# The second product of the MLP in seven half-size products, for the second chunk of the second to sixth batch too

## The chip, the core and the metric

The kernel runs on one NeuronCore of a Trainium2 chip. The core has five engines, each with its own in-order queue: TensorE (PE, matrix products and transposes, with its weight loads listed as PEld), VectorE (DVE), ScalarE (ACT), GpSimd (POOL) and SyncE (SP), which here only issues DMAs. Matrix products land in PSUM, a small memory from which DVE and ACT read, and everything else lives in SBUF. The metric is the device time of the kernel in microseconds (us). Every run is set against the median of the kernel before, 1778.69 us.

## What is computed

Two blocks, one after the other, all in 32-bit floating point.

```python
# top-k attention: 8 batches, 8 heads, 576 rows, head size 64
scores = scale * q @ k.T
kth    = 32nd largest score of each row
scores = where(scores >= kth, scores, -1e9)
x      = softmax(scores) @ v            # heads side by side: (8, 576, 512)

# Fourier mix and MLP
u  = x + real(fft(fft(x, axis=1), axis=2))
un = (u - mean(u)) / sqrt(var(u) + 1e-6)
out = u + relu(un @ w_ch1) @ w_ch2      # 512 -> 2048 -> 512
```

## The kernel before

**The main loop.** The attention works on tiles of 128 rows of one head (and one tile of 64 rows of both heads); there are 9 tiles for a pair of heads, 36 for a batch and 288 in all. The main loop (from L1589) makes one *program step* for a tile, so a batch is a round of 36 steps. In step i PE makes the scores of tile i+3, DVE finds the top 32 of tiles i and i+1 (four MAX8 and three MATCH_REPLACE8 on 576 columns for each tile, L446 and L448), POOL writes the tile's bounds (`nt`, L455), ACT and POOL mask the tile before (L469, L472), ACT takes the exponential (L480) and splits it in two planes (L493), SP writes the planes to DRAM and brings them back transposed (`PT`, L506 and L527), and PE multiplies them with v some steps later (`attend`, L585). What a step issues is put on each engine's queue in the order of the program, and no engine overtakes itself.

**The rest of a batch** runs under the attention of the next two. Take batch b. In steps 3 to 9 of the next round POOL folds its x (`near`, L762, is the last). In steps 10 and 12 PE makes the transform over tokens (`dft_tokens`, tile `yp`, L809), in steps 13 and 14 that over channels (`dft_channels`, tile `mp`, L860 and L864), and in steps 15 to 17 it transposes the normalised rows (`channels_first`, tile `tpu`, L948). ACT copies each of these out of PSUM (L834 to L847, L874, L951). From step 18 on the MLP of the batch is dealt out.

**The MLP as units.** `mlp_units` (L1041) makes a list of units: for each of two chunks of rows (chunk 0: tiles 0, 1 and the small tile 4, 320 rows; chunk 1: tiles 2 and 3, 256 rows) 16 units of the hidden layer (`hidden`, L1055, ACT writes `hT`, L1059), and then the second product. Each unit has a cost in us that the program gives it: 8 x rows / 1200 for a hidden unit, 1.75 for a part of the second product. When a batch's units arrive, `level` (L1562) looks for the step length at which what is free in the steps up to the next arrival holds all the units in the list; each step then takes units from the list, between its fixed work, up to that length (`some`, L1579). The units of a batch end just before the next arrival, in step 16 or 17 of the round after.

**The second product** has two forms. The *plain* form (`back`, L1075) takes a tile of 128 rows at a time: eight parts, each of two matrix products of 128 x 128 with 128 x 512, into a PSUM tile `cp` (L1082). For tile 2, ACT scales the result (L1108) and POOL adds it to x (L1110); for tile 3, DVE does both (L1096). The *seven-product* form (`fast`, L1155) treats two tiles together as a 2 x 2 matrix of blocks and replaces eight block products by seven (p1 to p7), each in two parts of four matrix products with 256 columns (`product`, L1254), into two PSUM tiles `cv` (p2, p5, p3) and `cw` (p1, p4, p6, p7). It needs sums of blocks. Those of the weights lie in DRAM and are brought into two quarters of the weight tile by `bring` (L976) as each product finishes, and the last two loads put the weights back. Those of `hT` are made as the products go along by `mix` (L1198): four mixes of two halves each, 128 x 512, in place in `hT`. The first mix is queued ahead of the products, the other three after p1 and p4. Results are scaled by ACT (L1225) and added by POOL (L1227), the last ones of each tile by DVE (L1211).

**Who does the sums, and when.** Mixes and adds go to a list `sums`. Up to the last tile they run on POOL. A step takes from the list what fits into 2.1 us less what is planned for POOL, then writes the bounds of its tile, and then takes what fits into another 1.3 us (`some_sums`, L1002). A planned fold counts 1.5 us, a mix 1.25. A product that needs a mix that was not yet issued issues it on the spot (`need`, L1009).

**PSUM banks.** `bank` (L144) turns three banks of the pool `ps_m`. A tile asked for with `hold` keeps its bank until its `free` is called; the others go round in what is left. Hidden units, `yp`, `mp` and `tpu` take a bank each without holding it (only in the last batch do `yp`, `mp` and `tpu` go to other pools); `cp`, `cv` and `cw` hold theirs. A plain tile's bank is freed when its result was read; `cv` is freed with DVE's add after p3, `cw` with that after p7.

```python
    def bank(shape, name, hold=False):
        n = banks_free.pop(0)
        t = ps_m.tile(shape, F32, name=name, tag=f"m{n}", bufs=1)
        if not hold:
            banks_free.append(n)
            return t
        return t, lambda: banks_free.append(n)
```

Before the change, the first batch has the plain form in both chunks, the second to sixth batch the seven products in the first chunk and the plain form in the second, and the last two batches the seven products in both. The small tile 4 is always plain.

Of the kernel before, what the change touches and what calls it, by code (L numbers as in the profile page):

```python
# [86 lines left out]
def kernel(  # L87
# [10 lines left out]
    B, H, S, D = q.shape  # L98
# [942 lines left out]
    def mlp_units(b):  # L1041
# [4 lines left out]
        def hidden(ch, it):  # L1046
            w, unT = CW[ch], unT_of[b, ch]
            if ch not in hTs:
                hTs[ch] = batp.tile([P, NIT, CW[0]], F32, name=f"hT_{b}_{ch}", tag="hT")
                hT_of[ch] = hTs[ch].rearrange("p i c -> p (i c)")[:, 0:NIT * w].rearrange(  # L1050
                    "p (i c) -> p i c", c=w
                )
            hp = bank([P, CW[0]], f"hp_{b}_{ch}_{it}")
            for dt in range(NDT):
                nc.tensor.matmul(  # L1055
                    hp[:, 0:w], lhsT=w1[:, dt, P * it:P * (it + 1)], rhs=unT[:, dt, 0:w],
                    start=(dt == 0), stop=(dt == NDT - 1),
                )
            nc.scalar.activation(out=hT_of[ch][:, it, :], in_=hp[:, 0:w], func=AF.Relu)  # L1059
# [275 lines left out]
        for ch in range(2):  # L1335
            units += [
                (8 * CW[ch] / 1200.0, lambda ch=ch, it=it: hidden(ch, it), ("hidden", b, ch))
                for it in range(NIT)
            ]
            seven = b and ch == 0 or b >= B - 2  # L1340
            if seven:
                begin, products = fast(ch)
                if ch == 0:
                    begins.append(begin)
                else:
                    units.insert(1 - NIT, (0.0, begin, ("hidden", b, 1)))
                mix_first = products.pop(0)
                units.append(mix_first)
            for t in [t for t in CHUNKS[ch] if t == 4 or not seven]:
                units += [  # L1350
                    (1.75, lambda ch=ch, t=t, p=p: back(ch, t, p), "back")
                    for p in range(4 if t == 4 else 8)
                ]
            if seven:
                units += products
# [127 lines left out]
    for b in range(B):  # L1483
# [49 lines left out]
        at(s + 1, "begin" if quick else "dve", lambda b=b: rsqrt(b))  # L1533
        arrivals.append(s + (1 if quick else 3))
        at(arrivals[-1], "units", lambda b=b: (queue if b else waiting).extend(mlp_units(b)))

    queue, waiting, pending, written, now, out_next = [], [], [], set(), [0], []
    step_us = 6.0

    def chunk_at(i):  # L1540

        for tile in (i - 5, i - 4, i - 3, i - 2):
            r = tile % PER_PAIR
            if PER_BATCH <= tile < N and r in (4, 8):
                if i - tile == ((5 if r == 4 else 4) if by_dma(tile) else 2 if tile in (2 * PER_BATCH - 1, N - 1) else 3):
                    return tile // PER_PAIR, r // 8
        return None, None
# [41 lines left out]
    while i < N + 5 or plan or queue or sums:  # L1589
# [96 lines left out]
        pair, ch = chunk_at(i)  # L1686
# [81 lines left out]
```

## Time and profile before

| | |
|---|---|
| median of 3 runs | 1778.69 us (1776.69 to 1779.95) |
| the profiled execution's own time | 1780.27 us |
| its span, first to last instruction | 1778.5 us |
| mean granted TensorE clock | 0.964 |
| PE, DVE, ACT, POOL busy | 1632.1, 1552.5, 1278.8, 906.6 us |
| one round in the steady state (1094 to 1287 us) | 193 us: PE 190.0, DVE 185.1, ACT 154.9, POOL 103.5 us busy |

The profile is of one execution. A group of instructions is shown as line, engine, operation, out<-in with sizes, count, then busy time, the mean duration of one in ns, and the idle time of the engine just before these with what ended it. A row of the timeline has start, duration, engine, line and count, and in brackets the engine's idle time before it. A matrix product in 32-bit floating point stands as two records in the trace. Busy time of a stage is read from windows given in us from the start of the span.

### The profile page before, as it was taken

To read this page: it belongs to the slowest core of one execution; us is meant where nothing else is said; L and a number is where in the kernel's file an instruction comes from. 1 tells how busy PE (TensorE), PEld (TensorE's weight loads), DVE (VectorE), ACT (ScalarE), POOL (GpSimd) and SP (SyncE) were. 2 spreads that over 40 slices of the span, in tenths; PEclk is the share of its full clock that TensorE was granted. 3 is DMA by queue.
4 is the path that set the end of the run, shared out by engine and by line. 5 is a ranking of instruction groups with operands and counts; after the bars stand their busy time and mean duration, and the time that the engine had idled before them with its cause. 6 is when DMAs were issued, how large, how long until landed. Compare 5 with 4: busy or idle time off the path is not lost.

```text
span 1778.5 us, 26295 instructions
## 1 busy us (share of the span) xinstructions
PE 1632.1 (92%) x7830; PEld 1040.9 (59%) x7830; DVE 1552.5 (87%) x3319; ACT 1278.8 (72%) x3136; POOL 906.6 (51%) x1268
## 2 busy tenths in 40 slices
PE   5666689999898989999999999999999999999998
PEld 3444455464455755566555755576566755577777
DVE  7999989999999999998999999999999999863121
ACT  6888759887787878876888778877978787653200
POOL 4768846655634565354544665356535564333000
PEclk7778799999999999999999999999999999999999
DMA  5333126651457855586557856595558655643151
GB/s 156 115 102 117 32 81 163 185 152 50 119 145 196 222 131 135 136 233 161 135 136 200 212 133 140 152 240 145 152 132 222 182 135 128 172 114 101 36 180 60
DMA packets 492926, 255.28 MB, mean 144 GB/s; under 512 B 364528, under 2 KB 483056, under 8 KB 492784
## 3 DMA queue, kind: packets, MB, share of 16 engines
q1 hardware_dynamic: 489008, 243.80, 52.5%
q0 software_dynamic: 2816, 9.44, 1.6%
q8 instruction: 63, 1.03, 0.2%
q14 instruction: 79, 0.65, 0.1%
q10 hardware_dynamic: 960, 0.36, 0.1%
HBM read 99.79 MB, written 84.74 MB: 104 GB/s over the span
## 4 chain that ended last, share of the span: by engine, by line
PE 48%; DVE 16%; ACT 16%; POOL 14%; issue 5%; DMA 2%; POOLq 0%; SPq 0%; DVEq 0%; ACTq 0%
PE hp L1055 18%; DVE m L446 7%; DVE wk L448 6%; PE o L585 6%; PE cw L1254 5%; POOL wk L472 5%; PE cv L1254 4%; PE sp L422 4%; ACT wk L469 3%; POOL fold L696 3%; PE cp L1120 2%; ACT wk L493 2%; PE cp L1082 2%; ACT S L425 2%; PE sp_t L392 1%
## 5 line engine op out<-in xcount | busy, mean ns | idle before, releaser
L472 POOL TENSOR_TENSOR wk<-S,wk 128x576 f32<-128x576 f32 x288 | 407.6, 1415 | 418.1 <-ACT wk L469 417.2
L446 DVE MAX8 m<-wk 128x8 f32<-128x576 f32 x864 | 617.4, 741 | 0.1
L1055 PE MATMUL hp<-unT,w 128*128 128x256 f32 (+1 forms) x2048 | 529.6, 409 | 6.8 <-ACT hT L1059 6.0
L1055 PEld LDWEIGHTS hp<-unT,w 128*128 128x128 f32 x2048 | 378.0, 191 | 112.0 <-ACT hT L1059 11.4
L448 DVE MATCH_REPLACE8 wk<-m,wk 128x576 f32<-128x576 f32 x576 | 424.8, 737 | 0.0
L469 ACT ACTIVATE wk<-S,nt 128x576 f32<-128x576 f32 x288 | 224.3, 779 | 96.8 <-POOL nt L455 96.3
L493 ACT COPY wk<-S 128x576 uint16<-128x576 uint16 x468 | 290.2, 673 | 0.0
L446 DVE MAX8 m<-S 128x8 f32<-128x576 f32 x288 | 214.5, 745 | 11.6 <-ACT S L396 11.6
L480 ACT ACTIVATE S<-wk,nt 128x576 f32<-128x576 f32 x234 | 185.1, 791 | 46.7 <-POOL wk L472 45.4
L448 DVE MATCH_REPLACE8 wk<-m,S 128x576 f32<-128x576 f32 x288 | 212.5, 738 | 0.0
L1082 PE MATMUL cp<-w,hT 128*128 128x512 f32 x448 | 206.0, 598 | 0.0
L1059 ACT ACTIVATE hT<-hp 128x320 f32<-128x320 f32 (+1 forms) x256 | 104.1, 411 | 140.7 <-PE hp L1055 139.7
L585 PE MATMUL o<-PT,v 128*64 128x256 f32 (+3 forms) x1440 | 196.1, 417 | 5.6 <-DVE wk L448 2.1
L422 PE MATMUL sp<-kT,qT 64*128 64x512 f32 (+1 forms) x528 | 160.1, 668 | 6.7 <-ACT S L414 3.6
L585 PEld LDWEIGHTS o<-PT,v 128*64 128x64 f32 x1440 | 113.2, 154 | 84.1 <-issue 24.8
L425 ACT COPY S<-sp 128x512 f32<-128x512 f32 (+1 forms) x264 | 141.7, 589 | 26.2 <-PE sp L422 25.2
L455 POOL TENSOR_TENSOR nt<-m,cc 128x2 f32<-128x2 f32 x288 | 58.7, 204 | 166.9 <-DVE m L446 160.4
L1254 PE MATMUL cw<-w,hT 128*128 128x256 f32 x512 | 119.7, 383 | 9.1 <-ACT ct L1225 6.2
L1082 PEld LDWEIGHTS cp<-w,hT 128*128 128x128 f32 x448 | 81.3, 193 | 75.1 <-issue 74.7
L392 PEld LDWEIGHTS sp_t<-kt,qT 128*128 128x128 f32 x320 | 51.7, 195 | 111.4 <-issue 73.3
L1254 PEld LDWEIGHTS cw<-w,hT 128*128 128x128 f32 x512 | 94.5, 190 | 27.3 <-ACT ct L1225 8.4
L1254 PE MATMUL cv<-w,hT 128*128 128x256 f32 x432 | 100.4, 383 | 6.6 <-DMA w<-w_parts 2.8
(155 smaller groups left out, 2036.3 us busy)
## 6 DMA issues: line engine op xcount, KB each, us to landing
planes<-wk SPq DMA_DIRECT2D x208, 288.0 KB, 2.7
w<-w_parts SPq DMA_DIRECT2D x94, 512.0 KB, 4.7
space<-in_moe_w_ch_dram SPq DMA_DIRECT2D x32, 512.0 KB, 3.6
nat<-in_q_dram SPq DMA_DIRECT2D x128, 64.0 KB, 2.3
v<-in_v_dram SPq DMA_DIRECT2D x32, 256.0 KB, 3.4
nat<-in_k_dram SPq DMA_DIRECT2D x62, 128.0 KB, 2.8
planes<-wk SPq DMA_DIRECT2D x52, 144.0 KB, 2.7
w_parts<-w_t POOLq DMA_DIRECT2D x8, 512.0 KB, 4.0
```

Of the source, the lines that this page charges most:

```text
L422: nc.tensor.matmul(sp[r], lhsT=qT[hd, q_cols], rhs=kT[hd, :], start=True, stop=True)
L425: nc.scalar.copy(out=s_t[r, keys], in_=sp[r])
L446: ops.append(lambda src=src, m8=m8: nc.vector.max(out=m8, in_=src))
L448: ops.append(lambda src=src, m8=m8: nc.vector.match_replace(w, m8, src, NEG))
L469: nc.scalar.activation(out=w, in_=Ssb[i], func=AF.Relu, scale=-FAR, bias=Nt[i][:, 1:2])
L472: nc.gpsimd.tensor_tensor(out=w, in0=Ssb[i], in1=w, op=ALU.subtract)
L480: nc.scalar.activation(out=Ssb[i] if by_dma(i) else w, in_=w, func=AF.Exp, bias=Nt.pop(i)[:, 0:1], accum_out=den_t[pair % 3][:, c:c + 1],)
L493: nc.scalar.copy(out=words[:, half, :], in_=src[:, half, :])
L585: nc.tensor.matmul(o[D * e:D * (e + 1), c0:c1], lhsT=vv[:, e, c, :], rhs=pt[:, NF if c == NF else (NF + 1) * e + c, c0:c1], start=(c == 0) ...
L1055: nc.tensor.matmul(hp[:, 0:w], lhsT=w1[:, dt, P * it:P * (it + 1)], rhs=unT[:, dt, 0:w], start=(dt == 0), stop=(dt == NDT - 1),)
L1082: nc.tensor.matmul(cp, lhsT=hT[:, it, P * n:P * (n + 1)], rhs=w2[:, it, :], start=(it == 0), stop=(it == NIT - 1),)
L1254: nc.tensor.matmul(dst, lhsT=h()[a][:, kc, :], rhs=rhs_of(kc), start=start and kc == 0, stop=kc == NK - 1, skip_group_check=True,)
```

## The change

One condition in `mlp_units` is changed. It decides for which chunks the seven-product form is used: before, for the first chunk of every batch but the first and for both chunks of the last two; after, for both chunks of every batch but the first. So the second chunk of the second to sixth batch changes form. Everything that `fast` issues for a second chunk comes with it: the loads at its start, placed after the chunk's first hidden unit, the first mix ahead of the products, the fourteen parts in place of sixteen, and the scratch room for scaled results in the unused end of `hT`.

```diff
@@ -1337,7 +1337,7 @@
                 (8 * CW[ch] / 1200.0, lambda ch=ch, it=it: hidden(ch, it), ("hidden", b, ch))
                 for it in range(NIT)
             ]
-            seven = b and ch == 0 or b >= B - 2
+            seven = b > 0
             if seven:
                 begin, products = fast(ch)
                 if ch == 0:
```

## The prediction

> **What bounds the kernel now.** I read the page first, for the shape of the whole span.
>
> ```profile
> PE 1632.1 (92%) x7830; PEld 1040.9 (59%) x7830; DVE 1552.5 (87%) x3319; ACT 1278.8 (72%) x3136; POOL 906.6 (51%) x1268
> ...
> PE   5666689999898989999999999999999999999998
> ...
> DVE  7999989999999999998999999999999999863121
> ...
> PEclk7778799999999999999999999999999999999999
> ```
>
> Two engines are nearly full from the sixth slice to the thirty-fifth, and PE alone after that. Which of them sets the pace is read from the busy time in single rounds of 193 us (one attention batch each), then in the 55 us in which the plain second chunk of the fifth batch runs.
>
> ```profile
> 1094.00:1287.00 193.00, 189.99 (x921) 118.70 (x920) 185.07 (x398) 154.86 (x379) 103.49 (x151) 1.00 0.65 168
> 1287.00:1480.00 193.00, 189.72 (x920) 118.60 (x919) 185.30 (x399) 154.18 (x378) 103.59 (x151) 1.00 0.65 166
> 1232.00:1287.00 55.00, 54.46 (x254) 28.00 (x253) 53.14 (x117) 48.01 (x122) 33.34 (x46) 1.00 0.56 142
> ```
>
> The columns are length, then busy time of PE, weight load, DVE, ACT and POOL, then clock. PE is idle 3.0 us of 193, DVE 7.9. The rounds repeat each other, so a steady state is reached. DVE's timeline says what its idle time is:
>
> ```profile
> 1222.01 0.42 DVE L630 TENSOR_TENSOR x<-tpx,rd 128x256 f32<-128x256 f32 x1 [0.58 <-PE tpx L626]
> ...
> 1257.85 0.76 DVE L446 MAX8 m<-S 128x8 f32<-128x576 f32 x1 [1.59 <-ACT S L396]
> ```
>
> Both are waits for work that PE issued (a transposed tile, a score block that ACT copies). So PE's in-order queue sets the round, and DVE meets it at a handful of places. A microsecond taken from or put into PE's queue counts, until DVE's 7.9 us are used up.
>
> **What the change takes away.** The groups by line give the arithmetic.
>
> ```profile
> L1082 PE MATMUL cp<-w,hT 128*128 128x512 f32 x448 | 206.0, 598 | 0.0
> ...
> L1254 PE MATMUL cw<-w,hT 128*128 128x256 f32 x512 | 119.7, 383 | 9.1 <-ACT ct L1225 6.2
> ...
> L1254 PE MATMUL cv<-w,hT 128*128 128x256 f32 x432 | 100.4, 383 | 6.6 <-DMA w<-w_parts 2.8
> ```
>
> A record costs PE 206.0/448 = 0.460 us at 512 columns and (119.7+100.4)/944 = 0.233 us at 256. The plain chunk is 64 records, 29.4 us; seven products are 7x16 = 112, 26.1 us. That is -3.3 us a batch, -16.6 us in five.
>
> **What it adds beside PE's path, a batch.** Eight POOL mixes of 1.28 us (62.5/49, L1198) and five adds of 0.73, less one add of 1.27: +12.6 us on POOL, busy 33.3 of the 55 us above. Five ACT scalings of 0.47 less one of 0.77: +1.6 us, into 48.0 of 55. On DVE a 256-wide add, +0.47 us, inside its 7.9. Twelve 512 KB loads: the SP queue spends about 0.6 us on one, 7 us a batch, and DMA is 0.56 busy there. I cost all this at nothing; the cover is those idle shares. The loads wait on SP for a product to end, with plane writes and transposes queued behind, but the operands are wanted two program steps (10 us) later. If a cover went, the dearest row is 2.8 us, PE's wait for w<-w_parts (once, second batch). The last store is issued one step later, so the four held transposed tiles go out in steps 22 to 25 instead of 20 to 24; four buffers hold them: nothing, at most DVE's longest wait there, 3.2.
>
> **Where the units fall.** The step level is that at which what is free in the 36 steps holds the batch's units. These cost 120.9 by the code's figures (34.1+27.3 hidden, 7 tail, 24.5, 28) and 117.4 after, so it falls by 0.1, from 5.24 to 5.14 us. Dealt out by hand, right to about one unit, the second chunk's hidden layer ends in step 6 with the first mix queued there; p2, p2, p5 in step 7; p5, p1 in 8; p1 in 9; p4 in 10; p4, p6 in 11; p6, p3 in 14; p3 in 15; p7, p7 in 16. That is the stretch of the next batch's token and channel transforms and the folds on POOL.
>
> **First wait added: p5 for the mix.** In the first chunk four tail units stand between the mix and p5; here only p2 does. POOL is late in these steps:
>
> ```profile
> 1236.58 0.19 POOL L455 TENSOR_TENSOR nt<-m,cc 128x2 f32<-128x2 f32 x1
> ...
> 1242.01 0.19 POOL L455 TENSOR_TENSOR nt<-m,cc 128x2 f32<-128x2 f32 x1
> ...
> 1248.21 2.14 POOL L762 TENSOR_TENSOR near<-fold 128x513 f32<-128x513 f32 x2
> ```
>
> These are the bounds of tiles 6 and 7. A step with a fold leaves room for one 1.25 us mix, behind the bounds. So the second mix half starts at 1242.2 plus 0.45 (the first half took a gap of 0.89) and ends at 1243.9. PE, from 1221.8: six hidden units of 1.77, a transpose of 0.5, score blocks 1.4, three product parts of 1.85, scores 1.4, is ready at 1241.3. It waits 2.7 us. One unit earlier or later gives 2.9 or 3.1 by the same sum; the lower end is 0.4, POOL's share in the first chunk. I take 2.7.
>
> **Second wait added: one bank.** `bank` has three PSUM banks. The plain chunk holds one at a time; seven products hold two (v from p2 to p3's add, w from p1 to p7's). In steps 8 to 16 the transforms then turn in a single bank: PE may not write the next group before ACT has read the last. The trace shows such a turn, hidden units right after p7 while both banks are held:
>
> ```profile
> 1191.02 1.89 PE L1055 MATMUL hp<-unT,w 128*128 128x256 f32 x8
> 1193.47 1.99 PE L1055 MATMUL hp<-unT,w 128*128 128x256 f32 x8 [0.56 <-ACT hT L1059]
> ```
>
> and how late ACT reads the transforms today, where a second bank hides it:
>
> ```profile
> 1252.54 0.51 PE L809 MATMUL yp<-fs,near 128*128 128x145 f32 x2
> ...
> 1254.86 0.38 ACT L834 COPY y<-yp 128x256 f32<-128x256 f32 x1
> ...
> 1255.57 0.43 ACT L834 COPY y<-yp 128x256 f32<-128x256 f32 x1
> ```
>
> The second half of the transform starts at 1252.5; ACT's reads of the first half end only as the second copy starts, 1255.6. With one bank that is a wait of 3.1. The same reading of the other adjacent pairs gives 2.5 (second token transform), 1.6 (channel transforms), 0.7, 1.6 and 0.4 (transposes): 10.0 in sum, the upper end. The lower end is ACT ready at once: twice 0.8, 0.8, 0.7, sum 3.1; a gain is excluded, as no bank is won. Walked on with PE already late by p5's wait: the transform's first half ends at 1255.5, ACT comes to it after score copies and xT at 1256.7, reads to 1257.4, wait 2.0; then ACT has caught up, 0.9, 0.9, 0.8 and none. 4.6, nearer the lower end because a late PE gives ACT time. Last, p6 follows p4 at once in the same bank: 0.6, as in the 0.56 of p4 after p1.
>
> **Sum.** -3.3 + 2.7 + 4.6 + 0.6 = +4.6 us a batch in the steady state (fourth to sixth batch: 13.8). The third keeps some idle time, 3.5. In the second, PE already idles 5.3 us in that stretch (2.96, 1.77, 0.58), half of which the new waits fill: 2.2. Total +19.5. The profiled execution took 1780.3, 1.6 above the median of 1778.7; on the median this is **1798**.
>
> **A rule weighed.** Around 826.7 the trace shows the clock at half for 3.4 us after PE idled 2.10 us, while idles of 2.8 and 3.0 us at 560 and 657 left it at 1.00.
>
> ```profile
> 826.70:830.10 3.40, 3.40 (x16) 1.77 (x14) 3.40 (x9) 0.82 (x3) 0.00 (x0) 0.51 0.52 83
> ```
>
> One such drop costs 1.7 us; one in three waits over 2 us, two of them a batch, adds 1.1 a batch, 6 in all. The Trainium skill, "TensorE: Matmul & The Clock Gate", section "Part 1: The HAM clock gate", says the clock halves only after a whole idle window of about 3.4 us. By that rule the waits above cost no clock; the 2.10 us row does not agree with it.
>
> **The rivals.**
> - *ACT stays late.* The bank waits are the 10.0 of today's alignment, p5's is 3.1, a clock drop adds 1.1: -3.3+3.1+10.0+0.6+1.1 = 11.5 a batch, with the same discounts (a factor of 0.85) +49: 1828. For it: ACT is 48 of 55 busy there. Against: ACT's own delays come partly from PE, which is late too.
> - *One bank costs nothing.* ACT reads in time; -3.3+2.7+0.6 = 0 a batch: 1779. Against: the copy at 1254.86. The Trainium skill, same page, section "HAM oscillation", reports a kernel in which PSUM double-buffering added nothing; by it this would be the outcome. The trace here disagrees at that copy.
> - *Faster.* The mixes come in time (0.4) and the banks cost 0.5 in all: -2.4 a batch, 1767. It decides where the new waits sum to less than 3.3 us, so that PE idles under 6.3 us a round. For it: seven products in the first chunk idle PE only about 1 us. Against: no transform runs there, and tails cover the mix.
>
> **Chances.** Forecast 0.62, ACT late 0.20, one bank free 0.09, faster 0.09. About 0.2% (3.6 us) is what a measurement tells from no change, so slower 0.82, same 0.09, faster 0.09. The forecast's own range, with waits of 6 to 10 us in place of 7.9, is 1790 to 1807; for 8 in 10 the range reaches to most of the late case and to the edge of no change: 1783 to 1830.
>
> **What would show it.** PE idle before the transforms (yp, mp, tpu), ended by ACT's y and us copies; PE before cv ended by POOL hT in steps 7 to 9; PE idle of about 11 us a round instead of 3; DVE's wait for S near step 12 grown by about 4 us; PE busy down 16 us. The prediction is wrong if the transforms show no wait, if the hold of the banks is shorter than read, or if PE's waits are made good because DVE or POOL paced the round.

## The result, and the profile after

The changed kernel takes 1821.02 us (median of 6 runs, 1815.97 to 1822.61) against 1779.32 us for the one before on the same chip (6 runs): a ratio of 1.0232 with a 95% interval of 1.0217 to 1.0247. That is 41.7 us slower. The forecast was slower, by 19.5 us, with 1821 inside its range; the rival "ACT stays late" had 1828.

From here on a difference between two traces is between profiled executions: span 1817.2 us after, 1778.5 before, so 38.7 us. The first line of the page after, and its groups of the products and of the mixes:

```profile
PE 1625.4 (89%) x8070; PEld 1089.5 (60%) x8070; DVE 1555.5 (86%) x3324; ACT 1291.1 (71%) x3156; POOL 965.9 (53%) x1328
...
L1254 PE MATMUL cw<-w,hT 128*128 128x256 f32 x832 | 198.8, 385 | 11.7 <-ACT ct L1225 4.2
...
L1254 PE MATMUL cv<-w,hT 128*128 128x256 f32 x672 | 163.3, 391 | 26.4 <-POOL hT L1198 9.2
...
L1198 POOL TENSOR_TENSOR hT<-hT 128x512 f32<-128x512 f32 x89 | 113.4, 1275 | 11.6 <-PE cw L1254 11.6
```

PE's busy time fell by 6.7 us and its idle time grew by 45.4 (span less busy: 146.4 before, 191.8 after). The forecast had -16.6 and +36.1. So both halves came out worse. The rounds say how. Below are the windows of two rounds after (columns as before the change: length, then busy time of PE, weight load, DVE, ACT, POOL, then clock). A round ends where the next round's first tile is taken up by DVE:

```profile
1005.00:1206.30 201.30, 189.01 (x970) 128.69 (x969) 186.52 (x400) 157.57 (x383) 115.76 (x165) 0.99 0.75 193
1206.30:1410.40 204.10, 189.02 (x970) 129.63 (x969) 186.65 (x401) 157.61 (x383) 116.35 (x166) 0.99 0.76 190
```

The same rounds of before took 195.4 and 193.5 us. PE is now idle 12.3 and 15.1 us in them, not 2.9 and 3.3 (the rounds of before, cut in the same way), and the clock is below 1.00. DVE and ACT have more idle time too, and POOL is at 57%, so none of them has become full. PE's own timeline in the fifth batch's second chunk, only the lines where it waits:

```profile
1261.28 5.41 PE L1254 MATMUL cv<-w,hT 128*128 128x256 f32 x16 [4.17 <-POOL hT L1198]
...
1277.55 0.51 PE L809 MATMUL yp<-fs,near 128*128 128x145 f32 x2 [1.70 <-ACT yt L847]
...
1285.30 1.97 PE L1254 MATMUL cw<-w,hT 128*128 128x256 f32 x8 [1.34 <-POOL nt L455]
...
1289.88 0.51 PE L809 MATMUL yp<-fs,near 128*128 128x144 f32 x2 [0.89 <-ACT yt L847]
...
1296.93 0.71 PE L860 MATMUL mp<-fd,y 128*128 128x128 f32 x4 [0.70 <-ACT us L874]
...
1303.65 0.63 PE L948 MATMUL tpu<-turns,x 128*128 128x128 f32 x4 [1.43 <-ACT us L874]
...
1306.69 0.63 PE L948 MATMUL tpu<-turns,x 128*128 128x128 f32 x4 [0.68 <-ACT unT L951]
...
1313.19 0.63 PE L948 MATMUL tpu<-turns,x 128*128 128x128 f32 x4 [0.55 <-ACT unT L951]
```

Every wait that the forecast named is there: p5's (the first line), the bank's (yp, mp, tpu, ended by ACT's copies out of PSUM), p6's (the third line). For p6's the profile names POOL's bounds, but these were done at 1284.5. What ends 0.1 us before PE starts, at 1285.20, is ACT's read of p4 out of bank w, in ACT's timeline:

```profile
1284.71 0.49 ACT L1225 ACTIVATE hT<-cw,gi 128x256 f32<-128x256 f32 x1
```

The first line of PE's timeline shows one thing more. The sixteen records take 5.41 us, where the same sixteen take 3.62 elsewhere. POOL's timeline before that line shows why p5 waited:

```profile
1259.17 0.68 POOL L696 TENSOR_TENSOR fold<-fold 128x254 f32<-128x254 f32 x1
1259.81 0.19 POOL L455 TENSOR_TENSOR nt<-m,cc 128x2 f32<-128x2 f32 x1
1259.95 1.27 POOL L1198 TENSOR_TENSOR hT<-hT 128x512 f32<-128x512 f32 x1
```

The first half of the mix stands behind folds and the bounds, and PE resumes when it ends. (The forecast had the second half there; it put the first into an earlier gap of POOL.) The windows of 3.41 us around that wait, and around a shorter one 17 us later, show the 5.41 (column before the DMA share: the granted clock):

```profile
1258.50:1261.91 3.41, 0.63 (x3) 0.58 (x4) 3.41 (x9) 1.88 (x4) 3.27 (x6) 1.00 0.98 280
1261.91:1265.32 3.41, 3.41 (x10) 2.66 (x9) 2.21 (x5) 1.99 (x7) 3.33 (x8) 0.50 0.69 230
...
1275.56:1278.98 3.42, 1.72 (x15) 1.31 (x12) 0.19 (x1) 2.01 (x11) 1.25 (x2) 1.00 0.34 107
1278.98:1282.39 3.41, 3.41 (x17) 2.42 (x17) 2.23 (x6) 3.36 (x12) 0.70 (x1) 1.00 0.99 161
```

In the first window PE is busy 0.63 us and in the next one the clock is 0.50; in the third it is busy 1.72 and the clock stays. Behind 400 us, leaving out the last moments, the trace of before has 4 such half-clock stretches of 3.41 us, that of after 11 (eight new ones, at 562, 648, 682, 706, 883, 1057, 1262 and 1593 us, and the one of before at 827 is gone). Seven more, at 1.7 us each, are 11.9 us of PE time. Six of the new ones, 10.2 us, stand directly behind new waits. The other two do not: those at 562 and 1593 us stand behind waits of products that the change leaves alone, and the trace of before is the only one of this case without a drop near 562 us. So some of the seven is the luck of one execution. With the arithmetic saved that is -16.6 + 11.9 = -4.7 of busy time against -6.7 measured.

The idle time can be sorted by what PE was about to do. All five rounds in which a changed chunk runs, in us, summed from the brackets in PE's timeline, the first five rows over the stretch of the products and transforms, the last over the whole rounds:

```
waits of PE before                              before   after
cv (p2, p5, p3)                                   0.0     18.6
cw (p1, p4, p6, p7)                               0.0      3.6
yp                                                1.8     16.6
mp                                                0.0      3.5
tpu                                               0.2     12.9
tpq, tpx, hp, sp (other waits of the rounds)     14.8      2.6
```

New waits of 53 us stand against 12 us of older ones that are gone because PE comes later to their places. DVE's timeline of the same stretch shows the other side: its wait for S has grown from 1.59 to 3.18 us (the forecast had about 4 more), and waits for ACT's `rd` and for POOL's sums of x are new:

```profile
1276.79 0.19 DVE L612 RECIPROCAL rd<-rd 128x6 f32<-128x6 f32 x1 [2.59 <-ACT rd L611]
1280.16 0.76 DVE L446 MAX8 m<-S 128x8 f32<-128x576 f32 x1 [3.18 <-ACT S L396]
...
1298.24 0.69 DVE L909 BATCH_NORM_STATS2 st<-x 128x6 f32<-128x512 f32 x1 [1.83 <-POOL x L898]
```

PE's waits before yp, mp and tpu and before cv are what the forecast said would show it. What it said of PE's idle time (11 us a round) is short by up to 4 us, and of PE's busy time (16 us less) wrong, mostly by the clock. So the reading to be tested: the single bank costs most, p5's mix next, and the clock adds to both. The rivals: that POOL's or SP's added work costs, that DVE holds the round, or that something else stands behind the mix.

### The profile page after: what moved, and what is told of

Read it like the earlier page. It is cut to its first block, busy times and chain, and to the rows that moved or that the text cites. A ratio compares the mean times of both kernels' runs of the same rounds, so it can differ in the third digit from the quotient of the medians.

```text
span 1817.2 us, 26942 instructions
## 1 busy us (share of the span) xinstructions
PE 1625.4 (89%) x8070; PEld 1089.5 (60%) x8070; DVE 1555.5 (86%) x3324; ACT 1291.1 (71%) x3156; POOL 965.9 (53%) x1328
## 4 chain that ended last, share of the span: by engine, by line
PE 55%; DVE 14%; ACT 12%; POOL 12%; issue 4%; DMA 2%; SPq 1%; POOLq 0%; DVEq 0%; ACTq 0%
PE hp L1055 19%; PE cw L1254 7%; PE o L585 7%; DVE m L446 6%; PE cv L1254 6%; DVE wk L448 6%; PE sp L422 4%; POOL wk L472 4%; POOL fold L696 3%; PE cp L1120 2%; ACT wk L469 2%; PE sp_t L392 2%; ACT wk L493 2%; POOL hT L1198 2%; PE yp L809 2%
## 5 line engine op out<-in xcount | busy, mean ns | idle before, releaser
L1254 PE MATMUL cw<-w,hT 128*128 128x256 f32 x832 | 198.8, 385 | 11.7 <-ACT ct L1225 4.2
L585 PE MATMUL o<-PT,v 128*64 128x256 f32 (+3 forms) x1440 | 197.9, 420 | 7.3 <-DMA PT<-planes 3.1
L1254 PE MATMUL cv<-w,hT 128*128 128x256 f32 x672 | 163.3, 391 | 26.4 <-POOL hT L1198 9.2
L1254 PEld LDWEIGHTS cw<-w,hT 128*128 128x128 f32 x832 | 154.5, 192 | 38.3 <-ACT ct L1225 6.2
L585 PEld LDWEIGHTS o<-PT,v 128*64 128x64 f32 x1440 | 114.6, 155 | 84.2 <-issue 25.5
L1254 PEld LDWEIGHTS cv<-w,hT 128*128 128x128 f32 x672 | 126.8, 195 | 52.9 <-issue 12.8
L1198 POOL TENSOR_TENSOR hT<-hT 128x512 f32<-128x512 f32 x89 | 113.4, 1275 | 11.6 <-PE cw L1254 11.6
```

Source lines behind the costliest of these rows:

```text
L585: nc.tensor.matmul(o[D * e:D * (e + 1), c0:c1], lhsT=vv[:, e, c, :], rhs=pt[:, NF if c == NF else (NF + 1) * e + c, c0:c1], start=(c == 0) ...
L1198: adder().tensor_tensor(out=v[dst][:, k], in0=v[a][:, k], in1=v[c][:, k], op=op)
L1254: nc.tensor.matmul(dst, lhsT=h()[a][:, kc, :], rhs=rhs_of(kc), start=start and kc == 0, stop=kc == NK - 1, skip_group_check=True,)
```

## The experiments

Each run was timed against the kernel before on the same chip. Times are medians; a ratio is to the kernel before, with its 95% interval.

### The two waits taken away, singly and together, and one put into the kernel before

The transforms are moved to other pools (`e1_pools`):

```diff
-        return ps_t.tile(shape, F32, name=name, tag="tp") if b == B - 1 else bank(shape, name)
+        return ps_t.tile(shape, F32, name=name, tag="tp") if b >= 2 else bank(shape, name)
```

and the same condition for `mp` (in `ps_s`) and `tpu` (in `ps_t`).

> The changed kernel, but from the third batch on the transforms (yp, mp, tpu) take their PSUM from the pools of the scores and of the transposed tiles instead of the three banks that the products use. Bank theory (the waits of the transforms for the last free bank are the dearest part): the waits of about 6.3 us a batch before yp, cw, mp and tpu go in the rounds of the third to sixth batch, so 20 to 28 us less than the changed kernel's 1821, about 1797; PE's wait before cv for the mix on POOL stays at 3 to 4 us a batch. Rival, POOL theory (the first mix is what costs, and all behind it follows from PE being late): the time falls by less than 8 us, above 1813, since the scores' and transposes' own buffers are then waited for instead.

Measured: 1793.41 us, ratio 1.0097 (1.0067 to 1.0126). PE's waits before yp and tpu are gone (16.6 to 0.0 and 12.9 to 0.4 us), the wait before cv is not (18.6 to 18.1). New waits of the move are 3.4 us before the transposes of the scores, and mp still waits 2.4. The time is the bank theory's number.

The order of the products (`e2_order`):

```diff
-                for f in (p2, p5, p1, p4, p6, *((p7, p3) if last and ch else (p3, p7)))
+                for f in (
+                    *((p2, p1, p5) if ch and b < B - 2 else (p2, p5, p1)),
+                    p4, p6, *((p7, p3) if last and ch else (p3, p7)),
+                )
```

> The changed kernel, but in the second chunk of the second to sixth batch p1, which needs no mix, comes before p5, which does. POOL theory: PE's wait before cv (2.7 to 4.2 us a batch) goes, and with it some of the half-clock stretches behind it: 15 to 25 us less than 1821, about 1800. Bank theory: w and v are held from about the same step as before, so the waits before yp, mp and tpu stay at about 6 us a batch, and what p5 no longer waits is partly waited for at the second mix or at yp: less than 10 us gained, above 1811.

Measured: 1809.19 us, ratio 1.0164 (1.0132 to 1.0196): 12 us gained, just outside both expectations and between them. The wait before cv halved (18.6 to 9.8 us), yp, mp and tpu kept theirs (17.7, 3.5, 12.9).

Both edits (`e3_both`).

> Both edits together: the transforms in other pools and p1 before p5. If the two waits and the half-clock stretches that follow them are all there is to the loss of 42 us, both gains add and the time is that of the kernel before or up to 10 us less (the arithmetic saved, 3.3 us a batch, remains): 1770 to 1785. If another cost is hidden in the change (POOL's 12.6 us a batch, DVE's waits for POOL's x, the twelve loads), it stays above 1790.

Measured: 1781.69 us, ratio 1.0013 (1.0000 to 1.0026). The two gains, 28 and 12, add to 40, and 39 were found. So the two waits make up nearly all of the 42 us. But of the 16.6 us of saved arithmetic nothing shows yet, so other costs of about that size remain.

One bank less in the kernel before (`e4_hold`):

```diff
                 cps[t] = bank([P, DM], f"cp_{b}_{t}", True)
+                if b and t == 2:
+                    kept.append(banks_free.pop(0))
...
                         free()
+                        if kept:
+                            banks_free.append(kept.pop())
```

> The kernel before, with its plain second chunk, but with one more of the three banks kept out of use from the second chunk's first tile to the end of its product, so that the transforms and hidden units turn in a single bank, as in the changed kernel; nothing else is changed. Bank theory: it costs 4.6 us a batch (the forecast) to 6.3 us (what the changed kernel's trace shows), and half-clock stretches on top, in some six rounds: 1805 to 1825. POOL theory: with PE not made late by the mix, ACT keeps up and a single bank costs under 1.5 us a batch: below 1788.

Measured: 1840.77 us, ratio 1.0345 (1.0317 to 1.0373), 61 us more than the kernel before and above both expectations. PE's timeline of this run in the fifth batch:

```profile
1291.64 0.51 PE L809 MATMUL yp<-fs,near 128*128 128x145 f32 x2 [3.13 <-ACT yt L847]
...
1303.43 0.51 PE L809 MATMUL yp<-fs,near 128*128 128x144 f32 x2 [1.97 <-ACT yt L847]
...
1312.11 0.71 PE L860 MATMUL mp<-fd,y 128*128 128x128 f32 x4 [0.70 <-ACT us L874]
```

The transforms wait 3.13 and 1.97 us here, where the changed kernel has 1.70 and 0.89. So the forecast's step from today's alignment to a smaller wait was right in kind: a PE that the mix has made late leaves ACT time, and a PE that comes on time waits the 3.1 that the forecast read off the trace of before. The idle time behind 400 us grew by 41.4 us, and twelve more windows at half clock than before came on top, 1.7 us each.

### Controls, the mixes, and p4 first

The same move of the transforms in the kernel before (`e5_before_pools`, edit as in `e1_pools`).

> The kernel before, with only the move of the transforms (from the third batch on) into the pools of the scores and of the transposed tiles. It is the control for the run with that move in the changed kernel, which gained 28 us. Bank theory: the plain chunk leaves two banks, so there is nothing to gain: 1776 to 1783. Rival: the move helps any kernel (another order of waits in the steps of the transforms): 1755 to 1772, and then the 28 us are not the price of the single bank.

Measured: 1789.45 us, ratio 1.0069 (1.0047 to 1.0090). Neither expectation: the move by itself costs 11 us. So the 28 us of `e1_pools` are net of a move that costs 11, and the price of the single bank lies between 28 and 28 + 11 = 39, if the move costs the changed kernel between nothing and what it costs the kernel before. That was not measured by itself.

The changed kernel without mixes in the second chunks (`e6_no_mix`):

```diff
             def mix(dst, a, c, op=ALU.subtract):
+                if ch and b < B - 2:
+                    summed.update((b, ch, dst, n) for n in range(2))
+                    return
                 v = h()
```

> The changed kernel without the four mixes (eight POOL instructions a batch) in the second chunk of the second to sixth batch, so that part of the sums of hT is left out there; products, loads and adds stay. Additive theory: what p5 waits for the mix goes (2.9 to 4.2 us in four or five batches, and the half-clock stretches behind these waits, some 5 us in all), with DVE's waits behind POOL: 1821 less 20 to 25 = 1796 to 1801. Rival, the banks take it over: without p5's wait ACT has less time before the transforms, whose waits grow from 6 to the 9.4 us a batch that the run with a bank kept back showed: only 5 to 10 us gained, 1811 to 1816.

Measured: 1816.18 us, ratio 1.0209 (1.0192 to 1.0226): 5 us gained, hardly clear of noise, since this interval and that of the changed kernel (1.0217 to 1.0247) overlap. The rival comes nearest, and PE's timeline in the fifth batch shows two things:

```profile
1262.60 3.72 PE L1257 MATMUL cv<-w,hT 128*128 128x256 f32 x16 [1.11 <-ACT hT L1228]
...
1278.38 0.51 PE L809 MATMUL yp<-fs,near 128*128 128x145 f32 x2 [2.90 <-ACT yt L847]
```

The first token transform waits 2.90 instead of 1.70, nearly as in `e4_hold`. And with no mix to wait for, p5 still waits, for an instruction that the forecast had not counted, ACT's scaling of p2's result (1.11 here, 3.45 and 2.55 in the second and sixth batch). It is in the ACT timeline of the same run:

```profile
1261.32 0.78 ACT L480 ACTIVATE S<-wk,nt 128x576 f32<-128x576 f32 x1 [0.39 <-POOL wk L472]
1262.00 0.19 ACT L480 ACTIVATION_READ_ACCUMULATOR S<-wk,nt 128x1 f32 x1
1262.09 0.45 ACT L1228 ACTIVATE hT<-cv,gi 128x256 f32<-128x256 f32 x1
```

p2 and p5 are two halves of one bank, v. PE writes the second half only after ACT has read the first. The Trainium skill, "PSUM — Partial Sum Buffer", section "PSUM bank collisions raise a hardware error", asks for such a guard: by bank and quadrant of partitions, not by address. The trace agrees, with the 1.11 us here; the forecast had counted this for p6 after p4 in bank w, but not for p5 after p2.

Both edits and no mixes (`e7_both_no_mix`).

> The run with both edits (1782), less the four mixes in the second chunk of the second to sixth batch (part of the sums of hT left out there). POOL theory: what is left of the loss, 18 us against the arithmetic saved, is POOL's load: DVE waits 3 to 5 us a round for POOL (the batch norm's x, the planes behind the adds) and PE 1 to 3 us for mixes: 1765 to 1772. Rival: DVE's own 185 us a round and its waits for PE's transposed tiles set the round, and PE's saved arithmetic can't be turned into time: 1778 to 1783.

Measured: 1790.95 us, ratio 1.0072 (1.0045 to 1.0098), above both expectations and not faster than `e3_both`. POOL's added work, 46 us less here in sum (920.1 against 965.9 in the changed kernel), is not what is left.

p4 ahead of p5 as well (`e8_p4`), order p2, p1, p4, p5, p6, p3, p7 with the transforms moved.

> The transforms in other pools, and in the second chunk of the second to sixth batch the order p2, p1, p4, p5, p6, p3, p7, so that two products instead of one stand between the first mix and p5. If PE's waits before cv (2.0 to 2.9 us a round with p1 alone in front) are what is left: 1770 to 1777, below the kernel before. Rival: the mixes are only later for p6 and p3, and DVE's waits behind POOL's queue stay: 1780 to 1786.

Measured: 1807.19 us, ratio 1.0167 (1.0149 to 1.0186), 25 us more than with p5 between p1 and p4. PE's timeline says what the expectation missed:

```profile
1242.98 3.78 PE L1254 MATMUL cw<-w,hT 128*128 128x256 f32 x8 [3.79 <-ACT hT L1225]
...
1267.09 3.33 PE L1254 MATMUL cw<-w,hT 128*128 128x256 f32 x7 [4.96 <-POOL x L1227]
```

p4 now follows p1 in bank w and waits 3.79 us for ACT's scaling. It is the same kind of wait as p5's after p2, made larger. p6 then waits 4.96 us, by the profile for a sum on POOL. In this kernel the order of the products has to alternate between the banks.

### One batch alone, p3 early, and the loads

Seven products in the second chunk of the fifth batch alone (`e9_one`):

```diff
-            seven = b > 0
+            seven = b and ch == 0 or b >= B - 2 or b == 4
```

> The kernel before, with the seven products in the second chunk of the fifth batch alone. If each batch pays for itself and nothing carries over: a fifth of 42 us, 8.3, and a half-clock stretch more or less (1.7): 1786 to 1789. If the rounds have to be late in a row for the loss to show (DVE's idle time of 8 us a round takes up one batch's waits): under 3 us, below 1782.

Measured: 1788.55 us, ratio 1.0047 (1.0032 to 1.0062), which is 8.4 us. Each batch pays for itself: 41.7/5 = 8.3.

p3 before p6 (`e10_p3`), and with yp moved (`e11_p3_yp`). With p3 early the rows of the first tile are stored ahead of p6's add, so that add is missing from the output of these two.

```diff
+                    (p2, p1, p5, p4, p3, p6, p7) if ch and b < B - 2 else
+                    (p2, p5, p1, p4, p6, *((p7, p3) if last and ch else (p3, p7)))
```

> The changed kernel with the second chunk's products of the second to sixth batch in the order p2, p1, p5, p4, p3, p6, p7: bank v comes free two parts earlier and p6 no longer follows p4 in the same bank. Bank theory: v is free before the second token transform, so of the waits (1.7 to 2.9 at the first, 0.9 to 2.1 at the second, 0.7, 1.4, 0.7, 0.6) those from the second on go, some 4 to 5 us a batch, and p5's as in the run with p1 in front: 1809 less 15 to 22 = 1787 to 1794. Rival: p3 then waits for the third mix on POOL instead (two mixes of 2.6 us lie before it) and holds the bank through that: 1803 to 1812.

> The run with p3 early, and of the transforms only those over tokens (yp, from the third batch on) in the pool of the transposed tiles. The move of all the transforms cost the kernel before 11 us by itself; a part of it should cost less. If the early p3 frees the bank for mp and tpu, this has no wait for a bank left and a smaller price for the move: 1772 to 1780. If the move of yp is what costs the 11 us (the score transposes then wait for ACT's yt, 0.5 us a round): 1782 to 1788.

Measured: 1821.28 us, ratio 1.0221 (1.0198 to 1.0244), and 1804.90 us, ratio 1.0139 (1.0122 to 1.0157). Both are worse than expected. In `e10_p3` the transforms of the fifth batch wait 1.71, 0.89, 0.70, 1.07 and 0.68 us, nearly what they wait with p3 late: v did not come free in time to help them. With p3 gone from between them, p7 follows p6 in bank w and waits 0.56, and preparations behind it wait 1.2 more.

No loads of weight sums in the second chunks (`e12_no_loads`):

```diff
-    def bring(o, place, part):
+    def bring_in(o, place, part):
...
+            skip = ch and b < B - 2
+
+            def bring(o, place, part):
+                if not skip:
+                    bring_in(o, place, part)
```

> The changed kernel without the twelve loads of weight sums in the second chunk of the second to sixth batch, so the products there use the plain quarters of the weights and the result is another sum. The forecast put the loads at nothing: 1815 to 1823. Rival: the SP queue is held by them (plane writes and transposes queue behind), and PE's new waits for the transposed planes in steps 4 and 5 (0.7 to 2.4 us a round) and DVE's for planes in step 11 (1.2 to 1.5) come from it: 1806 to 1812.

Measured: 1813.88 us, ratio 1.0186 (1.0168 to 1.0203), against the changed kernel's 1.0232 (1.0217 to 1.0247), between the two expectations. So the loads cost about 7 us, 1.4 a batch, where the forecast had nothing. Where, is only partly seen: the two profiled spans differ by 2.2 us, and the one wait that shows it is PE's for the transposed planes (L585, idle 7.3 us after and 4.7 without the loads).

### p2's wait for the last hidden unit

In the third and fourth batch the dearest wait before cv is not p5's (the text on record for `e13_swap` counts rounds, from zero). PE's timeline of the changed kernel, and then ACT's:

```profile
1050.22 3.19 PE L1254 MATMUL cv<-w,hT 128*128 128x256 f32 x14
1056.28 0.70 PE L1254 MATMUL cv<-w,hT 128*128 128x256 f32 x2 [2.88 <-ACT hT L1059]
```

```profile
1055.10 0.78 ACT L480 ACTIVATE S<-wk,nt 128x576 f32<-128x576 f32 x1 [0.38 <-POOL wk L472]
1055.78 0.19 ACT L480 ACTIVATION_READ_ACCUMULATOR S<-wk,nt 128x1 f32 x1
1055.87 0.36 ACT L1059 ACTIVATE hT<-hp 128x256 f32<-128x256 f32 x1
```

Sixteen records are p2. It stops two records before its end, because its last block of `hT` is the last hidden unit, and ACT writes that only after an exponential that waits for POOL's mask. The plain form reads the last unit only in the eighth part of a tile, where p2 reads it in its second. `e13_swap` makes units 8 to 15 first, `e14_both_swap` adds this to `e3_both`, `e15_best` leaves mp in the banks, and `e16_before_yp_tpu` is that smaller move in the kernel before.

```diff
-                for it in range(NIT)
+                for it in ((*range(NK, NIT), *range(NK)) if ch and 0 < b < B - 2 else range(NIT))
```

> The changed kernel, with the hidden units of the second chunk of the second to sixth batch in the order 8 to 15, then 0 to 7, so that p2, which reads units 8 to 15 at once, no longer needs the last one. In the changed kernel PE waits 2.9 us for it in the fourth and fifth round. If that is a price of its own: 1821 less 5.8 and two half-clock stretches of 1.7, so 1812 to 1816. Rival, the next waits take it over (p5 behind ACT's read of p2 in the same bank, or the mix): the wait moves from p2 to p5 and the time stays at 1817 to 1823.

> The run with the transforms in other pools and p1 before p5 (1782), with the hidden units in that order too. PE's two waits of 2.9 us before p2 go and p1 still stands before p5: 1782 less 6 to 9 = 1773 to 1776, below the kernel before. Rival, DVE paces the round (its idle time is already that of the kernel before, 5 to 10 us a round): 1779 to 1784.

> As the run before it, but the channel transforms (mp) stay in the three banks, where with the token transforms and transposes gone they have the free bank to themselves. In the scores' pool mp waited 0.8 us for ACT's score copy each round: 3 to 4 us less than the run before it, 1769 to 1773. Rival: the move of mp cost nothing on the whole, and it takes the same time within 2 us.

> Control: the kernel before with that smaller move alone (yp and tpu in the pool of the transposed tiles, mp in the banks). The move of all three cost it 11 us. If mp in the scores' pool was the price: 1777 to 1782. If the price lies in the pool of the transposed tiles (score transposes wait 0.5 us a round for ACT's yt): 1785 to 1791.

Measured: `e13_swap` 1820.89 us, ratio 1.0234 (1.0214 to 1.0254), no gain. The wait has moved to p5, whole, in PE's timeline of that run:

```profile
1060.03 4.21 PE L1254 MATMUL cv<-w,hT 128*128 128x256 f32 x9 [4.19 <-POOL hT L1198]
```

`e14_both_swap` took 1778.81 us, ratio 0.9991 (0.9978 to 1.0005), 3 us less than `e3_both`, with intervals that overlap. `e15_best` took 1781.28, ratio 1.0008 (0.9998 to 1.0018). `e16_before_yp_tpu` took 1784.67, ratio 1.0023 (1.0013 to 1.0033), so the smaller move costs 4 us where the larger cost 11. No version was faster than the kernel before by more than the measurement tells.

### Does DVE hold what is left?

In `e14_both_swap` PE has 16.6 us less arithmetic than the kernel before and takes the same time. The same work was taken from DVE in both (`e17_before_dve`, and `e18_swap_dve` on `e14_both_swap`):

```diff
         for r in rounds:
...
+            if r == 2 and 3 * PER_BATCH <= i < 7 * PER_BATCH and i % 9 in (2, 6):
+                continue
```

> The kernel before with DVE relieved: in 8 of the 36 tiles of a round, in the rounds of the fourth to seventh batch, the third MATCH_REPLACE8 is left out (0.74 us and its value load of 0.07 each, so 6.5 us a round and 26 in all; these tiles then use a larger bound than the 32nd score). If PE's queue alone sets the round before the change, the time falls by less than 8 us, above 1772. If DVE sets it as much as PE, by 12 to 26 us.

> The run with all three edits (transforms in other pools, p1 before p5, hidden units 8 to 15 first; 1779 us), with DVE relieved in the same way. If DVE holds the round once PE's waits are gone, so that PE's saved arithmetic (3.3 us a batch, 13 in these four rounds) can't show, this relief brings it out: 13 to 26 us less, 1753 to 1766, and more than the same relief brings the kernel before. If what is left is in PE's own waits, it falls by less than 8 us, above 1771, as the kernel before does.

Measured: 1776.04 us, ratio 0.9985 (0.9973 to 0.9996), and 1781.55 us, ratio 1.0006 (0.9989 to 1.0023). DVE's busy time fell by 21.5 us in the one (1552.5 to 1531.0) and by 18.0 in the other (1553.3 in `e14_both_swap`, 1535.3 here). This gave 3 us in the one and nothing in the other. DVE does not hold the round, before or after. What is left is in PE's own queue, here in the fifth batch of `e14_both_swap`:

```profile
1237.40 1.99 PE L1254 MATMUL cv<-w,hT 128*128 128x256 f32 x8 [0.75 <-POOL hT L1198]
...
1241.22 1.99 PE L1254 MATMUL cv<-w,hT 128*128 128x256 f32 x8 [1.27 <-POOL hT L1198]
...
1250.09 0.49 PE L392 MATMUL sp_t<-kt,qT 128*128 128x128 f32 x2 [0.53 <-ACT yt L847]
...
1256.40 1.97 PE L1254 MATMUL cw<-w,hT 128*128 128x256 f32 x8 [0.90 <-POOL nt L455]
```

These four waits, 3.45 us, use up the 3.3 us that the batch saves. (The last ends, as p6's above, with ACT's read of p4 out of bank w.) Over the whole span the account closes: -16.6 of arithmetic, +10.8 of idle time behind 400 us (60.4 against 49.6), and two half-clock windows (+3.4), -2.4 in sum; the spans differ by -1.6 (1776.9 and 1778.5).

## Why the prediction was right or wrong

The direction and both mechanisms were right, and the size was less than half: +41.7 us against +19.5. The step that failed is "A rule weighed": the half-clock stretches behind the new waits were seen and priced, at 6 us in all, and then stand in the sum at nothing. In the traces they took 10.2 to 11.9 us. The second is the size of the waits themselves, 7.9 us a batch ahead of the discounts, where cv, cw, yp, mp and tpu waited 53 us more in five batches, 10.6 each. That the result lies inside the range owes to the rival of late ACT, for whose sake the range reaches to 1830; the forecast's own range ended at 1807.

- **The bound: right.** PE's queue sets the round. The runs with DVE relieved show it for both kernels.
- **The arithmetic, -16.6: right to about 2 us**, and hidden in the changed kernel's busy time by the clock. `e18_swap_dve` has as much half-clock time behind the first 408 us as the kernel before, and there PE's busy time is 14.3 us less (1301.8 against 1316.1).
- **Costed at nothing: right for POOL, ACT and DVE, wrong for the loads.** POOL's busy time grew by 59.3 us (forecast 63), ACT's by 12.3 (8) and DVE's by 3.0 (2.4). Taking the mixes away from the repaired kernel gained nothing. The twelve loads a batch, for which the forecast named cover on SP and in DMA, cost about 7 us in all.
- **The dealing: right to about one unit.** In the fifth batch p4 and the first part of p6 stand between the two token transforms, p3 and p7 among the transposes.
- **First wait, 2.7 a batch: short by 1.0, incomplete in cause.** Measured were 18.6 us before cv in five batches, 3.7 each. The forecast sent PE past p2 at once and put the whole wait down to the mix. Three things stand in a row there: p2's last block of `hT` (2.9 us in the third and fourth batch), ACT's read of p2 out of the bank that p5 writes, and the mix (up to 4.2). Taking one away leaves the others: about 5 us for the mix, none for p2's block, 12 for putting p1 in between, which covers the last two.
- **Second wait, 4.6 a batch: the mechanism is shown, the size was short.** yp, mp and tpu wait 31 us more in five batches, 6.2 each. The walk forecast 2.0, 0.9, 0.9 and 0.8; the fifth batch has 1.70, 0.89, 0.70 and 2.66. The step of the walk that failed is "then ACT has caught up": the three tpu waits are 1.43, 0.68 and 0.55, not one of 0.8, and in the second to fourth batch the second wait for yp is 2.1, not 0.9. `e1_pools` shows the price from one side, at least 28 us with the clock's part, and `e4_hold` from the other.
- **p6 after p4, 0.6 a batch: right on average only.** cw waits 3.6 us in five batches, 0.7 each. But p6 waits 1.3 us in the fifth and sixth batch and not at all in the others; in the second it is p4, after p1, that waits 0.9.
- **The discounts for the second and third batch: wrong.** Rounds grew by 8.6, 4.4, 5.9, 10.6 and 11.4 us where 2.2, 3.5 and three times 4.6 were forecast. In the second batch the new waits did not fill PE's older idle time: idle grew by 6.5 us, and three half-clock windows came on top.
- **The clock, left out of the sum: the largest miss.** Seven more half-clock stretches took 11.9 us, six of them, 10.2 us, directly behind new waits. The forecast had the row at 826.7, priced one drop in three waits at 6 us, and then kept this for the rival alone. With idle time +45.4 against +36.1, the miss of 19 us between the traces (38.7 less 19.5) is 11.9 from the clock and 9.3 from the waits, less 2.0 of busy time. A rest of this size can come from the two executions: in the first 408 us, where the kernels do the same, PE's busy time already differs by 3.1 us (316.0 before, 312.9 after), with the clock at 0.86 and 0.88.
- **The rivals.** "ACT stays late" came nearest in time (1828), but its bank waits of 10.0 a batch were not reached, not even in `e4_hold`, where yp, mp and tpu wait 38 us more than before in five batches, 7.6 each; the change came near its time by smaller waits and more clock. "One bank costs nothing" and the section of the Trainium skill named beside it do not hold here: the second buffer is worth 28 us or more. "Faster" needed p5 and the banks to wait under 3.3 us a batch; only `e14_both_swap` came near that, at the time of the kernel before.

## What to carry to other kernels

A form that multiplies less but holds one more accumulator takes a buffer away from all other work of its stage; price that by the copies that empty the buffer, as they lie in the trace, before counting the products. For each product write down every release in a row in front of it (last operand, reader of the same bank, helper sum): taking one away gains only down to the next. Price short idles of PE with the clock that follows them.

## What was not expected of the hardware

**The clock looks at PE in fixed windows.** In each of the twenty traces of this case, all half-clock stretches behind 400 us (but the one at the very end, when PE has stopped) begin on one grid of 3.413 us, to within 0.0003 of a window. Summing PE's idle time in each window of that grid from 400 us to PE's last product, over all twenty traces, and asking whether the next window was at half speed:

```
PE idle in a window at full clock    windows   next one at half clock
under 1.7 us                          7772        2
1.7 to 1.9 us                           50       10
1.9 us or more                         141      136
in a window already at half clock:
under 0.3 us                           136        0
0.3 to 0.7 us                           24       12
0.7 us or more                          18       18
```

So an idle of 1.9 us that falls into one window nearly always costs 1.7 us more, the same idle split by the border between two windows costs nothing, and in a window already slow half a microsecond can keep it slow (the double stretches in `e4_hold` and `e6_no_mix`). This explains what the forecast could not: the 2.10 us before 826.7 that dropped the clock and the 2.8 and 3.0 us at 560 and 657 that did not, where no window holds more than 1.66 us of idle time. A wait of 2.7 us, the forecast's for p5, laid anywhere on this grid, has 1.9 us in one window in 1 - (2 x 1.9 - 2.7)/3.41 = 68% of positions. By that, an estimate from these counts, this wait alone should have been given about 1.2 us a batch. Where the grid lies differs from one execution to the next (the drop near 562 us begins between 558.8 and 564.2 us in nineteen traces), so a wait can drop the clock in one and not in another.

The Trainium skill, "TensorE: Matmul & The Clock Gate", section "Part 1: The HAM clock gate", says that the window is 3413 ns long and free-running. The traces agree. It also says that the clock falls after an idle window; here 1.9 us of 3.41 is enough.
